# Sums of tokens on another engine and in another block, seven products from block 2 on, later ends, and a weight scale from ScalarE

## The chip, the cores and the metric

The kernel runs on one core of a Trainium2 chip. Five engines work side by side, each with a queue of its own, and wait for one another through semaphores: TensorE (PE; the profile lists its weight loads as PEld), VectorE (DVE), ScalarE (ACT), GpSimd (POOL) and SyncE (SP), which here issues DMA transfers. The metric is the device time of one execution in microseconds, lower is better; the time before is the median of three runs.

## What is computed

With `xn` the rows of `x` brought to mean 0 and variance 1 (2048 tokens, 576 features), the output is `x`, plus the real part of a Fourier transform of `xn` over both axes, plus a two-layer network with 4608 hidden units:

```python
xn = _layernorm(x, axis=-1)
a = jnp.einsum("bsd,ed->bse", xn, dft_hid_re)
b = jnp.einsum("bsd,ed->bse", xn, dft_hid_im)
y = jnp.einsum("ts,bse->bte", dft_seq_re, a) - jnp.einsum("ts,bse->bte", dft_seq_im, b)
h = jnp.maximum(jnp.einsum("bsd,df->bsf", xn, w1), 0)
return x + y + jnp.einsum("bsf,fd->bsd", h, w2)
```

All is float32. The kernel forms each float32 product from three float16 products: an operand is scaled by a power of two and split into an upper half (`hi`, rounded to float16) and a lower half (`lo`, the rest), and `hi*hi + hi*lo + lo*hi` is added up.

## The kernel before

**Stages.** The network comes first, then the Fourier transform over the features (`dft1`), then that over the tokens (the loop over `units` at the end). The change touches the network alone.

**Tiling of the network.** The hidden units are cut into 9 blocks `b` of 512, the tokens into 4 groups `g` of 512. A step is one pair `(b, g)`; `steps` lists them block by block, and step number `n` is the place in that list. In each step the loop forms the first layer of `(b, g)` and beside it the second layer of the step before (`mlp2`, seven products `n` = 0 to 6 of a scheme that gets a 2x2 block product from seven multiplications instead of eight; each is 12 matmuls of 128x288).

**First layer, two ways.** In block 0 `mlp1_step` forms it plainly: 13 matmuls of 128x512 for each of four slices, and four more on half the rows. `mlp1_out` (L340 to L359) then takes two slices out of PSUM and makes the seven left operands `h` that the second layer reads, among them four sums `S1` to `S4`, each split into halves (L358 on ScalarE, L359 on VectorE). From block 1 on `pair_products` (L413) forms the first layer with seven products as well, `P1` to `P7`, for `first` and `second`, the two halves of a block's hidden units; a product is 6 or 8 matmuls of 128x256. Its function `behind` (L445) does what follows a product: PSUM is read by ScalarE or VectorE, `value` (L440) makes a pair of halves, and after `P4` the ends follow: the upper halves of the sums on ScalarE (L468) and the lower halves on VectorE (L469). The four PSUM banks `banks1` are written in turn, so a product must wait until the one before it in its bank has been read (L447, L452, L454).

**Sums of tokens.** The seven products need sums of halves of `xn` transposed (`xT`). `sums_x` (L389) is a generator that makes four such sums for a group with GpSimd instructions of 128x512 (L400 to L404 and L409) and a ScalarE copy (L407). It writes them over `acc` of the group, which held the output of block 0 until that was sent to DRAM (`spill<-acc`, L515). `tq` strings the generators of the four groups together, and the loop advances it a piece at a time in steps 2 to 5.

**Weights.** `prepare_block(b)` gives a list of small pieces of work for the next block (load, scale, split and sums of `w1` and `w2`); `work()` takes one piece from it. The scale of `w1` comes from the greatest magnitude: two reductions on VectorE for each half (`max_w1`, L113, and L531), then `power`, where GpSimd takes the greatest over the partitions (L119), or in blocks 0 and 1 `power_pe`, which does the same with small matmuls (L156). The scale of `w2` comes from a sum of magnitudes that ScalarE forms in one instruction (`sum_w2`, L585). `split` (L178) has an upper half on ScalarE (L180) and a lower half on VectorE (L181). For blocks past 0, `split_w1b` and `sums_w1` (L568 to L572) make the sums of `w1` that the seven products need.

**Output of the second layer.** ScalarE copies four of the seven products into one of three buffers (L507; the buffers are called `sum` and `dbuf` in the profile), VectorE adds the other three (L509), and GpSimd's queue issues the transfers that add a buffer to DRAM (L511). In block 0 VectorE adds all of them into `acc`.

**Passes.** From step 6 on the loop also runs `passes`: a load of a 512 KB tile `f` of the Fourier matrices (one buffer) and its sum of magnitudes on ScalarE (L846). They are for the scales of the last stage.

**Order.** The framework places instructions: it takes the order of the program text and moves an instruction ahead where its inputs are planned to be there; `tc.issue_after` ties one to another. On each engine the order is then fixed, and an instruction that waits holds up all behind it.

The seven products' schedule in a step, with the places at which work, sums and passes are called:

```python
            for k, (do, q) in enumerate((
                (first, P1), (first, P2), (m, 0), (first, P5), (first, P6), (m, 1), (second, P1),
                (first, P7), (m, 2), (second, P2), (first, P3), (first, P4), (m, 3), (second, P6),
                (m, 4), (second, P5), (second, P7), (m, 5), (m, 6), (second, P3), (second, P4),
            )):
```

Of the kernel before, what the change touches and what calls it, by code (L numbers as in the profile page):

```python
# [38 lines left out]

NW1 = 17  # L40
W1B = NW1 * P
EXPONENT = 0x7F800000
SX = 4.0
EPS = 1e-5
# [3 lines left out]
def kernel(  # L48
# [340 lines left out]
    def sums_x(g):  # L389

        f = mlp.tile([P, 2, 2, GH], F32, tag="first", name=f"t{g}", bufs=1)
        tt = nc.gpsimd.tensor_tensor
        for q, (head, tail) in enumerate((
            ((0, 1), (0, 0)), ((1, 1), None), ((1, 0), None), ((1, 1), (0, 1)),
        )):
            t = f[:, q % 2]
            h, l = halves(g, head)
            if tail:
                h2, l2 = halves(g, tail)
                tt(t, h, h2, ALU.subtract)  # L400
                tt(t, t, l2, ALU.subtract)
            else:
                tt(t, h, f[:, 1 - q % 2], ALU.subtract)
            tt(t, t, l, ALU.add)  # L404
# [4 lines left out]
            tt(lo, t, hi, ALU.subtract)  # L409

    banks1 = []

    def pair_products(b, g, i):  # L413

# [30 lines left out]
        def behind(n):  # L445
# [5 lines left out]
            elif n == P6:  # L451
                nc.scalar.activation(s1, u, AF.Copy)  # L452
            elif n == P5:
                nc.scalar.activation(c22, w, AF.Copy)  # L454
            elif n == P7:
                tt(c22, u, c22, ALU.add)  # L456
                value(A22, c22)
            elif n == P3:
                tt(r21, w, s1, ALU.add)
                nc.scalar.activation(r21, r21, AF.Relu)  # L460
                stt(s3, c11, 0.0, r21, ALU.max, ALU.subtract)
                stt(s1, c22, 0.0, r21, ALU.max, ALU.add)
                stt(s2, c22, 0.0, s3, ALU.max, ALU.subtract)
            elif n == P4:
                value(A12, u)
                stt(s4, u, 0.0, s2, ALU.max, ALU.subtract)  # L466
                hi, lo = (h[:, k, S1 : S4 + 1] for k in range(2))
                order["s"] = nc.scalar.activation(hi, st[:, 1:], AF.Copy).ins  # L468
                order["lo"] = nc.vector.tensor_tensor(lo, st[:, 1:], hi, ALU.subtract).ins  # L469

        def run(n):
            product(n)
# [46 lines left out]
    def max_w1(b, f):  # L519
# [3 lines left out]
            mx["w1", b], sc["w1", b], pw["w1", b] = cell("mw1"), cell("sw1"), cell("pw1")  # L523
        if r == 0:
            mx["f", b] = cell("mf", 2)
            mx["b", i] = small.tile([P, 1], BF16, tag=f"mb{i}", name=f"mb{b}_{i}") if b < 2 else None
        with tc.issue_after(order["acc" if b > 1 else "lo"]) if b else nullcontext():
            magnitude(mx["f", b][:, r : r + 1], raws["w1", b, i][:, r * KT : (r + 1) * KT])
        if r:
            m = mx["w1", b][:, i : i + 1] if b > 1 else mx["b", i]  # L530
            nc.vector.tensor_reduce(m, mx["f", b], AX.X, ALU.max)  # L531

    def later(step):

# [2 lines left out]

    def power_w1(b, i):
        s, p = (t["w1", b][:, i : i + 1] for t in (sc, pw))
        if b > 1:  # L540
            yield from power(s, p, mx["w1", b][:, i : i + 1])
        else:
            power_pe(s, p, mx["b", i])

    def split_w1(b, f):
        i, r = divmod(f, 2)
        k = slice(r * KT, (r + 1) * KT)
        if r == 0:
            w = w1bufs[i].bitcast(F16)[:, : 4 * KT * P]
            w1s[b, i] = w.rearrange("p (n k f) -> p n k f", n=2, f=P)  # L550
        w = w1s[b, i]
        split(w[:, 0, k], w[:, 1, k], raws["w1", b, i][:, k], sc["w1", b][:, i : i + 1])

    def split_w1b(b, i, c):

        if c == 0:
            w = w1bufs[b % 2 * 2 + i].bitcast(F16)
            w1s[b, i] = w.rearrange("p (n k f) -> p n k f", n=2, f=P)
        w, r = w1s[b, i], raws["w1", b, i]
        src = (r[:, :5], r[:, 7:], r[:, :5], r[:, 5:9])[c]  # L560
        k = (slice(0, 5), slice(5, 8), slice(8, 13), slice(13, 17))[c]
        split(w[:, 0, k], w[:, 1, k], src, sc["w1", b][:, i : i + 1])

    def sums_w1(b, i):
        r = raws["w1", b, i]
# [288 lines left out]
    for n in range(2, len(steps)):  # L854
# [16 lines left out]
        if b == NB - 1 and g == 1:  # L871
# [51 lines left out]
    mlp.release()  # L923
# [214 lines left out]
```

## Time and profile before

| | |
|---|---|
| median of three runs | 1365.46 us (1365.22 to 1368.71) |
| the profiled execution | 1367.02 us |
| its span | 1364.9 us |
| mean granted TensorE clock | 0.974 |
| block 0, up to step 4 | 0 to 140.05 us |
| block 1 (steps 4 to 7) | 140.05 to 255.51 us |
| blocks 2 to 8 (steps 8 to 35) | 255.51 to 904.45 us |
| both Fourier stages | 904.45 to 1364.9 us |

The stage borders are the starts of matmuls: that of the first product of a step, which is the first matmul of L435 in it. A row of the view by windows gives a stretch, its length, and for each engine the busy time and the number of instructions, then the granted clock of TensorE as a share of full speed, the busy share of the DMA engines, and GB/s. A row of the timeline gives start and duration in microseconds, engine, line, operation and tiles, and in brackets how long the engine had been idle and what ended that. A row of the groups gives the count, the total busy time and the mean duration in ns, then the idle time ahead of those instructions by releaser. A row of the waits gives the total, the number of times and the longest.

### The profile page before, as it was taken

The page shows a single profiled execution, that of the slowest core. Times are in us where ns is not written, and L with a number is a line of the kernel's source. Part 1 is how long each engine was busy: PE and PEld are TensorE (multiplying, and loading weights), DVE is VectorE, ACT ScalarE, POOL GpSimd, SP SyncE. Part 2 cuts the span into 40 slices and gives each one's busy share as a digit, 9 for nine tenths or more (in the row PEclk, how much of TensorE's full clock was granted, in tenths as well). Part 3 has the DMA queues.
Part 4 walks back from the last instruction along what each step waited for, and adds up shares of the span by engine and source line. Part 5 has one row for each costly group of instructions (what it writes and reads, how often), then busy time and mean ns, then how long its engine had stood idle before and what let it go on. Part 6 is the DMA issues. An engine that isn't in the chain of part 4 may idle for free.

```text
span 1364.9 us, 25952 instructions
## 1 busy us (share of the span) xinstructions
PE 1270.6 (93%) x10572; PEld 1023.3 (75%) x10572; DVE 1030.5 (76%) x1911; ACT 725.1 (53%) x1226; POOL 221.1 (16%) x244
## 2 busy tenths in 40 slices
PE   8878689999998999999989999999999999999998
PEld 7654467877877778778778778776777777777777
DVE  8968888677766777877677678648667878788785
ACT  6734346666665576676565666535443433333342
POOL 2466541111111112111111111120000000000000
PEclk8899899999999999999999999999999999999999
DMA  5111225566656647575656676442004443443420
GB/s 213 40 44 53 87 72 98 126 145 142 123 125 147 119 107 158 123 155 115 140 130 119 129 151 150 61 64 82 4 1 146 156 138 101 150 132 115 159 80 18
DMA packets 60807, 150.77 MB, mean 110 GB/s; under 512 B 6288, under 2 KB 21136, under 8 KB 60688
## 3 DMA queue, kind: packets, MB, share of 16 engines
q1 hardware_dynamic: 42256, 111.36, 25.1%
q0 software_dynamic: 18432, 37.76, 19.9%
q8 instruction: 82, 1.34, 0.4%
q14 instruction: 37, 0.30, 0.1%
HBM read 101.91 MB, written 47.19 MB: 109 GB/s over the span
## 4 chain that ended last, share of the span: by engine, by line
PE 43%; issue 18%; DVE 16%; DMA 11%; ACT 6%; POOL 4%; SPq 0%; POOLq 0%; ACTq 0%; DVEq 0%
PE p L1072 23%; PE p L498 7%; PE pd L958 6%; PE bank L435 6%; DMA spill<-dbuf 4%; DVE w2s L181 2%; POOL spill L511 2%; DMA spill<-sum 2%; DMA f<-in_cim_dram 2%; ACT f L846 1%; DVE h L443 1%; DMA c<-in_cre_dram 1%; DMA f<-in_cre_dram 1%; ACT j L585 1%; DVE h L469 1%
## 5 line engine op out<-in xcount | busy, mean ns | idle before, releaser
L498 PE MATMUL p<-w2s,h 128*128 128x288 f16 x3024 | 423.8, 293 | 28.9 <-DVE sum L509 9.3
L498 PEld LDWEIGHTS <-h 128*128 128x128 f16 x3024 | 302.1, 100 | 112.1 <-issue 32.5
L1072 PE MATMUL p<-R,cs 128*128 128x288 f16 x2688 | 331.1, 287 | 2.9 <-DVE o L1078 2.9
L1072 PEld LDWEIGHTS <-cs 128*128 128x128 f16 x2688 | 263.6, 98 | 70.2 <-issue 3.1
L180 ACT ACTIVATE cs<-c,sc_c 128x1024 f16<-128x1024 f32 x112 | 128.8, 1151 | 198.5 <-PE p L1072 152.4
L435 PEld LDWEIGHTS <-dbuf 128*128 128x128 f16 x1600 | 158.5, 99 | 48.5 <-issue 24.8
L435 PEld LDWEIGHTS <-w1buf 128*128 128x128 f16 x1600 | 157.2, 98 | 40.2 <-issue 18.6
L181 DVE SCALAR_TENSOR_TENSOR cs<-c,sc_c,cs 128x1024 f16<-128x1024 f32 x112 | 143.7, 1283 | 46.8 <-ACT cs L180 46.7
L435 PE MATMUL bank<-acc,dbuf 128*128 128x256 f16 x768 | 107.7, 277 | 21.0 <-ACT s L452 20.8
L435 PE MATMUL bank<-acc,w1buf 128*128 128x256 f16 x768 | 105.9, 275 | 15.7 <-ACT s L452 15.6
L511 POOL DMA_DIRECT2D spill<-dbuf x74 | 66.4, 922 | 331.7 <-DVE dbuf L509 327.7
L435 PE MATMUL bank<-xT,dbuf 128*128 128x256 f16 x832 | 112.3, 276 | 0.9 <-DVE s L466 0.9
L435 PE MATMUL bank<-xT,w1buf 128*128 128x256 f16 x832 | 110.4, 274 | 0.7 <-ACT acc L454 0.7
L958 PE MATMUL pd<-dbuf,xT 128*128 128x288 f16 x832 | 104.3, 286 | 1.6 <-DVE R L987 1.3
L469 DVE TENSOR_TENSOR h<-s,h 128x1024 f16<-128x1024 f32 x64 | 78.5, 1226 | 31.0 <-ACT h L468 30.9
L958 PEld LDWEIGHTS <-xT 128*128 128x128 f16 x832 | 80.7, 98 | 25.5 <-issue 5.5
L468 ACT ACTIVATE h<-s 128x1024 f16<-128x1024 f32 x64 | 67.6, 1056 | 46.4 <-DVE s L466 46.1
L507 ACT ACTIVATE dbuf<-p,c_ub 128x576 f32<-128x576 f32 x74 | 54.4, 735 | 50.8 <-PE p L498 23.7
L442 ACT ACTIVATE h<-acc 128x256 f16<-128x256 f32 x128 | 52.3, 409 | 51.8 <-DVE acc L456 47.6
L846 ACT ACTIVATE f<-f 128x1024 f32<-128x1024 f32 x64 | 66.9, 1045 | 14.6 <-DMA f<-in_cim_dram 9.6
L443 DVE SCALAR_TENSOR_TENSOR h<-acc,h 128x256 f16<-128x256 f32 x128 | 55.4, 433 | 25.1 <-ACT h L442 22.8
L1078 DVE SCALAR_TENSOR_TENSOR o<-p,us_c,o 128x288 f32<-128x288 f32 x112 | 57.5, 514 | 20.4 <-PE p L1072 20.2
(151 smaller groups left out, 1540.9 us busy)
## 6 DMA issues: line engine op xcount, KB each, us to landing
spill<-dbuf POOLq DMA_DIRECT2D x74, 288.0 KB, 5.1
f<-in_cre_dram SPq DMA_DIRECT2D x32, 512.0 KB, 3.8
f<-in_cim_dram SPq DMA_DIRECT2D x32, 512.0 KB, 3.7
c<-in_cre_dram SPq DMA_DIRECT2D x32, 512.0 KB, 4.6
c<-in_cim_dram SPq DMA_DIRECT2D x32, 512.0 KB, 4.8
spill<-sum POOLq DMA_DIRECT2D x38, 288.0 KB, 5.0
raw_w<-in_w_dram SPq DMA_DIRECT2D x17, 640.0 KB, 6.0
raw_w<-in_w_dram SPq DMA_DIRECT2D x18, 576.0 KB, 6.0
```

Source lines behind the costliest of these rows:

```text
L180: nc.scalar.activation(hi, src, AF.Copy, scale=s)
L181: nc.vector.scalar_tensor_tensor(lo, src, s, hi, ALU.mult, ALU.subtract)
L435: nc.tensor.matmul(ps, l, r, start=first and m == 0, stop=m == len(todo) - 1, skip_group_check=not first,)
L443: stt(lo, src, 0.0, hi, ALU.max, ALU.subtract)
L468: order["s"] = nc.scalar.activation(hi, st[:, 1:], AF.Copy).ins
L469: order["lo"] = nc.vector.tensor_tensor(lo, st[:, 1:], hi, ALU.subtract).ins
L498: nc.tensor.matmul(ps[:, c], h[:, x, qa, c * P : (c + 1) * P], w[:, y, qb], start=first and i == 0 and j == 0, stop=i == NQ - 1 and j == 2 ...
L511: nc.gpsimd.dma_start(spill[g, row, col], o, accum_op=ALU.add)
L846: nc.scalar.activation(f, f, AF.Abs, scale=2.0**-10, accum_out=sums_c[:, n, q : q + 1])
L958: nc.tensor.matmul(ps[j], xT[g][:, kx, c * P : (c + 1) * P], dsp[j][:, hl, k], start=(t % 2 == 0 and n == 0), stop=(t % 2 == 1 and n == le ...
L1072: nc.tensor.matmul(ps, w[:, a, k], r[:, c, rq], start=first and k == 0 and j == 0, stop=k == HK - 1 and j == 2, skip_group_check=not first,)
L1078: nc.vector.scalar_tensor_tensor(o, ps, us["c"][:, n : n + 1], o, ALU.mult, ALU.add)
```

## The change

Five things are altered.

- `sums_x` runs on VectorE instead of GpSimd. It is advanced in block 1's steps, eight pieces a step, and the rest in the first step of block 2. (In the order that the framework makes of it, 22 of the 56 instructions stand among the last two groups of block 0, 34 in block 1.)
- Block 1 uses the plain first layer of block 0; the seven products begin with block 2 (`BB`). So `w1` of block 1 is split like that of block 0, without sums, and its scale still comes by `power_pe`.
- The ends of a pair's sums are put on a list, `ends`, and taken from it after places 2, 4, 12 and 14 of the schedule: for `first` in the same step behind `m` 3 and `m` 4, for `second` in the next step behind `m` 0 and `P6`.
- From block 2 on, the scale of `w1` comes from a sum of magnitudes of a whole half (128x1280) on ScalarE, whose by-product is written to the buffer that the split fills later. The two reductions and the small one on VectorE go.
- `work()` is called at other places of the schedule (ten times a step as before; twice for each slice in block 1), and the passes begin in step 9, at places 9 and 18 of every step and 14 of odd ones.

```diff
+BB = 2
...
     def sums_x(g):
...
-        tt = nc.gpsimd.tensor_tensor
+        tt = nc.vector.tensor_tensor
...
-    banks1 = []
+    banks1, ends = [], []
...
                 stt(s4, u, 0.0, s2, ALU.max, ALU.subtract)
-                hi, lo = (h[:, k, S1 : S4 + 1] for k in range(2))
-                order["s"] = nc.scalar.activation(hi, st[:, 1:], AF.Copy).ins
-                order["lo"] = nc.vector.tensor_tensor(lo, st[:, 1:], hi, ALU.subtract).ins
+                ends.extend((end_hi, end_lo))
+
+        hi_s, lo_s = (h[:, k, S1 : S4 + 1] for k in range(2))
+
+        def end_hi():
+            order["s"] = nc.scalar.activation(hi_s, st[:, 1:], AF.Copy).ins
+
+        def end_lo():
+            order["lo"] = nc.vector.tensor_tensor(lo_s, st[:, 1:], hi_s, ALU.subtract).ins
...
+    def sum_w1(b, i):
+
+        if i == 0:
+            mx["w1", b], sc["w1", b], pw["w1", b] = cell("mw1"), cell("sw1"), cell("pw1")
+        w = w1bufs[b % 2 * 2 + i].bitcast(F16)
+        w1s[b, i] = w.rearrange("p (n k f) -> p n k f", n=2, f=P)
+        nc.scalar.activation(
+            w[:, : 2 * KT * P].rearrange("p (k f) -> p k f", f=P), raws["w1", b, i], AF.Abs,
+            scale=2.0**-10, accum_out=mx["w1", b][:, i : i + 1],
+        )
...
     def prepare_w1(b, i):
         p = power_w1(b, i)
+        if b < BB:
+            return [
+                lambda: max_w1(b, 2 * i),
+                lambda: max_w1(b, 2 * i + 1),
+                lambda: later(p),
+            ], [
+                lambda: split_w1(b, 2 * i),
+                lambda: split_w1(b, 2 * i + 1),
+            ]
         return [
-            lambda: max_w1(b, 2 * i),
-            lambda: (max_w1(b, 2 * i + 1), b > 1 and next(p)),
+            lambda: (sum_w1(b, i), next(p)),
+            lambda: None,
             lambda: later(p),
...
-        if b:
+        if b >= BB:
             first, second = (pair_products(b, g, i) for i in range(NQ))
...
                 do(q)
-                if k % 2:
+
+                if k in (2, 4, 12, 14) and ends:
+                    ends.pop(0)()
+                for _ in range({2: 1, 3: 1, 5: 1, 8: 1, 9: 1, 12: 1, 13: 1, 16: 1, 18: 2}.get(k, 0)):
                     work()
-                if n < 6:
-                    k % 2 or next(tq, None)
-                elif k in (5, 11, 20) and (k != 5 or n % 3 == 0) and passes:
+                if n == 2 + NG * BB - 2 and k in (5, 9, 13, 18):
+                    next(tq, None)
+                if n > NG * BB and (k in (9, 18) or k == 14 and n % 2) and passes:
                     passes.pop(0)()
...
-            if g + 1 < NG:
+            if b == 0 and g + 1 < NG:
...
-            for _ in range(3):
+            for _ in range(1 if b else 3):
                 work()
             for q in range(2 * i, min(2 * i + 2, 7)):
                 mlp2(pb, pg, q)
-                for _ in range(2 if q > 3 and n == 2 or q < 2 and n == 3 else n - 2):
+                if b:
                     next(tq, None)
-            for _ in range(3):
+            if b and i == 3:
+                next(tq, None)
+            for _ in range(1 if b else 3):
                 work()
...
     for q in range(7):
         mlp2(*steps[-1], q)
+        if ends:
+            ends.pop(0)()
```

More of the change, by code (lines that the diff above doesn't have):

```diff
@@ L525, in max_w1 @@
             mx["f", b] = cell("mf", 2)
-            mx["b", i] = small.tile([P, 1], BF16, tag=f"mb{i}", name=f"mb{b}_{i}") if b < 2 else None
-        with tc.issue_after(order["acc" if b > 1 else "lo"]) if b else nullcontext():
+            mx["b", i] = small.tile([P, 1], BF16, tag=f"mb{i}", name=f"mb{b}_{i}")
+        with tc.issue_after(order["lo"]) if b else nullcontext():
             magnitude(mx["f", b][:, r : r + 1], raws["w1", b, i][:, r * KT : (r + 1) * KT])
         if r:
-            m = mx["w1", b][:, i : i + 1] if b > 1 else mx["b", i]
-            nc.vector.tensor_reduce(m, mx["f", b], AX.X, ALU.max)
+            nc.vector.tensor_reduce(mx["b", i], mx["f", b], AX.X, ALU.max)
     def later(step):
@@ L539, in power_w1 @@
         s, p = (t["w1", b][:, i : i + 1] for t in (sc, pw))
-        if b > 1:
+        if b >= BB:
             yield from power(s, p, mx["w1", b][:, i : i + 1])
@@ L548, in split_w1 @@
         if r == 0:
-            w = w1bufs[i].bitcast(F16)[:, : 4 * KT * P]
+            w = w1bufs[b % 2 * 2 + i].bitcast(F16)[:, : 4 * KT * P]
             w1s[b, i] = w.rearrange("p (n k f) -> p n k f", n=2, f=P)
@@ L554, in split_w1b @@
     def split_w1b(b, i, c):
-        if c == 0:
-            w = w1bufs[b % 2 * 2 + i].bitcast(F16)
-            w1s[b, i] = w.rearrange("p (n k f) -> p n k f", n=2, f=P)
         w, r = w1s[b, i], raws["w1", b, i]
@@ L877 @@
             ]
-        if b:
+        if b >= BB:
             first, second = (pair_products(b, g, i) for i in range(NQ))
```

## The prediction

> **What bounds the kernel now.** I read the page first, then busy time by stage, then single steps, then who waits for whom. The profiled execution took 1367.0 us, of which its span is 1364.9; the three timed runs have a median of 1365.5.
>
> ```profile
> span 1364.9 us, 25952 instructions
> PE 1270.6 (93%) x10572; PEld 1023.3 (75%) x10572; DVE 1030.5 (76%) x1911; ACT 725.1 (53%) x1226; POOL 221.1 (16%) x244
> ```
>
> TensorE (PE) is the engine to watch, but its 93% is an average. The cuts by stage are: the last two token groups of block 0, block 1, blocks 2 to 8, and the Fourier part. Columns: window, its length, busy time of each engine (instructions), granted clock, DMA share, GB/s.
>
> ```profile
> 75.50:140.00 64.50, 52.20 (x342) 32.49 (x341) 45.65 (x75) 26.43 (x44) 42.53 (x36) 0.92 0.19 66
> 140.05:255.51 115.46, 95.34 (x741) 75.49 (x739) 95.98 (x182) 60.12 (x116) 43.31 (x38) 0.91 0.40 93
> 255.51:904.45 648.94, 609.81 (x5154) 508.32 (x5152) 475.96 (x1044) 410.58 (x795) 105.99 (x136) 0.98 0.60 126
> 904.45:1364.90 460.45, 450.27 (x3670) 354.95 (x3667) 344.37 (x425) 181.58 (x199) 3.82 (x5) 1.00 0.32 98
> ```
>
> The same view by step (one block and one token group), the first three steps of block 1, the first of block 2 and one late step:
>
> ```profile
> 140.05:177.71 37.66, 27.06 (x190) 19.93 (x188) 35.06 (x59) 15.51 (x29) 19.45 (x15) 0.82 0.21 62
> 177.71:209.04 31.33, 25.16 (x186) 19.59 (x184) 26.61 (x50) 14.87 (x29) 16.39 (x14) 0.89 0.34 79
> 209.04:233.89 24.85, 21.69 (x186) 17.98 (x184) 19.37 (x48) 17.49 (x33) 3.80 (x6) 1.00 0.45 87
> 255.51:276.82 21.31, 21.31 (x187) 18.00 (x185) 17.62 (x40) 14.38 (x28) 3.05 (x6) 1.00 0.50 99
> 815.08:836.28 21.20, 21.20 (x186) 18.01 (x184) 16.76 (x31) 12.82 (x25) 3.63 (x6) 1.00 0.67 138
> ```
>
> A step of seven products without a stall takes 21.20 us: PE is busy throughout. So blocks 2 to 8 (28 steps, floor 28 x 21.20 = 593.6) lose 55.3 us, 9.3% of the floor, and block 1 (floor 84.8) loses 30.7 in four steps. There VectorE (DVE) fills 35.06 of 37.66 and 26.61 of 31.33, just where GpSimd (POOL) works 19.45 and 16.39. Its instructions are longer there, too:
>
> ```profile
> 182.76 1.22 POOL L403 TENSOR_TENSOR t<-xT,t 128x512 f32<-128x512 f16 x1
> 184.06 1.21 POOL L404 TENSOR_TENSOR t<-t,xT 128x512 f32<-128x512 f32 x1
> 182.89 1.38 DVE L462 SCALAR_TENSOR_TENSOR s<-acc,s 128x256 f32<-128x256 f32 x1
> 184.19 1.37 DVE L463 SCALAR_TENSOR_TENSOR s<-acc,s 128x256 f32<-128x256 f32 x1
> 187.17 0.41 DVE L466 SCALAR_TENSOR_TENSOR s<-bank,s 128x256 f32<-128x256 f32 x1
> ```
>
> L462 and L463 read two SBUF tiles and end 0.29 us behind a POOL instruction (184.27 against 183.98, 185.56 against 185.27), after 1.38 and 1.37; L466, of the same size, reads PSUM and takes 0.41. Then the waits of PE, the first four from 75 to 255 us, the others from 255 to 905 (total, times, longest):
>
> ```profile
> PE bank L435 <- ACT s L452: 12.7, 5, 7.4
> PE pm L156 <- DVE mb L531: 4.6, 1, 4.6
> PE p L498 <- ACT xT L266: 4.6, 1, 4.6
> PE p L498 <- DVE c_sw L123: 2.9, 1, 2.9
> ...
> PE bank L435 <- ACT s L452: 23.6, 19, 3.3
> PE p L498 <- DVE dbuf L509: 7.6, 4, 1.9
> PE p L498 <- DVE sum L509: 6.9, 5, 1.8
> ```
>
> **The change part by part.** *PE's work in block 1.* Eight products come back: per step 52 matmuls of 128x512 and 4 on half the rows, instead of 100 of 128x256; the 84 of 128x288 stay.
>
> ```profile
> 65.48 6.20 PE L308 MATMUL p<-xT,w1buf 128*128 128x512 f16 x28
> 113.62 0.61 PE L333 MATMUL p<-xT,w1buf 64*128 64x512 f16 x4
> 370.73 1.91 PE L435 MATMUL bank<-xT,dbuf 128*128 128x256 f16 x16
> 372.48 1.63 PE L498 MATMUL p<-w2s,h 128*128 128x288 f16 x12
> ```
>
> One matmul lasts about 0.38, 0.27 and 0.29, so the starts lie (6.20 - 0.38)/27 = 0.216, (1.91 - 0.27)/15 = 0.109 and (1.63 - 0.29)/11 = 0.122 apart. A step costs 52 x 0.216 + 0.4 + 84 x 0.122 = 21.9 against 100 x 0.109 + 84 x 0.122 = 21.2: +0.7 a step, **+2.8** in all, and block 1's floor is 87.6.
>
> *Sums of tokens, from POOL to VectorE.* 56 instructions of 128x512 (14 a group).
>
> ```profile
> L409 POOL TENSOR_TENSOR acc<-t,acc 128x512 f16<-128x512 f32 x16 | 22.4, 1405 | 32.0 <-ACT s L348 11.7 <-DVE s L459 10.1 <-DMA spill<-acc 8.5
> L248 DVE TENSOR_TENSOR dbuf<-dbuf 128x512 f16<-128x512 f32 x1 | 0.7, 684 | 0.0
> L352 DVE SCALAR_TENSOR_TENSOR h<-p,h 128x512 f16<-128x512 f32 x8 | 5.5, 681 | 1.6 <-ACT h L351 1.5
> L181 DVE SCALAR_TENSOR_TENSOR w1buf<-raw_w,c_sw,w1buf 128x640 f16<-128x640 f32 x20 | 18.8, 946 | 3.7 <-ACT w1buf L180 3.7
> ```
>
> At L248's 0.684 they are 38 us of VectorE; at POOL's own 1.405 it would be 79, and I take the first, the same engine and size. In the built order 22 of them stand among block 0's last two groups, 34 in block 1. VectorE in a step of block 1 then has: outputs 2 x (0.41 + 0.68 + 4 x 0.41 + 1.22) = 7.9, sums 34/4 x 0.684 = 5.8, three L509 at 0.81 = 2.4 (1.22 and 0.81 are L469's and L509's rows below), and a quarter of block 2's weights, 32 instructions between L466's 0.41 and L181's 0.95, about 5. That is 21.1 by durations, some 18 by starts (L466's successor starts 0.34 behind it, not 0.41): 83% of 21.9, the share that the step at 255.51 carries (17.62 of 21.31) with 0.1 lost. So I give block 1 the loss of blocks 2 to 8, 9.3%: 87.6 x 1.093 = 95.7 instead of 115.5, **-20**. Ends: no loss, -28; the 17% of the step at 209.04 (24.85 over 21.2), 102.5, -13.
>
> The rule that weighs here is the Trainium skill's, page "TensorE: Matmul & The Clock Gate", section "What's actually happening": PE falls to half clock after about 3.4 us of idleness, so a shorter new stall costs only itself. The trace differs: the step at 177.71 has a granted clock of 0.89 and PE busy for 25.16, though its longest wait is the 2.9 us for c_sw. By the rule block 1's remaining 8 us would be waits alone, by the row up to half as much again, 4 us; both lie inside the ends above.
>
> *Block 0's last groups.* VectorE gets 22 x 0.684 = 15.0 there, loses the sums of block 1's w1 and half its splits (about 6.7), and what it waited for POOL. Two PE waits have POOL behind them: ScalarE's copies to xT stand behind L407, which waits for POOL's t, and mb L531 stands behind VectorE's long instructions. Of these 9.2 us I count half, **-5**; ends -11 and +8 (VectorE's net 15.0 - 6.7 on the path).
>
> The sums' last instruction, L411 now, also brings VectorE a wait that POOL had: for spill<-acc to land, 8.5 us in all on the sixteen L409. Behind it in VectorE's queue stand the outputs and L509s that PE waits for. The same on VectorE would cost up to 8.5; in the built order five other instructions and one transfer lie between block 0's last add and the first L411, as on POOL, so I count nothing and keep 8.5 within block 0's upper end.
>
> *Ends made later, in blocks 2 to 8.* In the built order ScalarE's h is hardly moved, but VectorE's lower half now stands behind L509 where it stood ahead of it:
>
> ```profile
> 413.21 1.22 DVE L469 TENSOR_TENSOR h<-s,h 128x1024 f16<-128x1024 f32 x1
> 414.34 0.81 DVE L509 SCALAR_TENSOR_TENSOR dbuf<-p,c_ub,dbuf 128x576 f32<-128x576 f32 x1
> 415.21 1.63 PE L498 MATMUL p<-w2s,h 128*128 128x288 f16 x12 [1.91 <-DVE dbuf L509]
> ```
>
> PE waits 1.91 for an L509 with 1.22 of L469 ahead of it. Nine such waits make 14.5; 1.1 off eight of them is **-9**. What is late next is h itself, first read by the third product of the next step, several us later.
>
> *w1's scale.* Seven blocks lose 28 L113 and 14 small reductions on VectorE and gain 14 sums of 128x1280 with a read each on ScalarE.
>
> ```profile
> L113 DVE TENSOR_REDUCE c_mf<-raw_w 128x1 f32<-128x640 f32 x36 | 29.0, 808 | 0.6 <-DMA raw_w<-in_w_dram 0.5
> L585 ACT ACTIVATE j<-raw_w 128x1152 f32<-128x1152 f32 x16 | 18.7, 1168 | 1.1 <-DMA raw_w<-in_w_dram 0.5 <-DVE h L469 0.4
> L585 ACT ACTIVATION_READ_ACCUMULATOR j<-raw_w 128x1 f32 x16 | 3.1, 197 | 0.0
> ```
>
> VectorE: 28 x 0.81 + 14 x 0.15 = 24.7 less. ScalarE: 1.168 x 1280/1152 + 0.197 = 1.49, x14 = 20.9 more, at 410.58 of 648.94 busy; an idle third covers it, and were it all on the path it would cost 20.9. The 23.6 us in which PE waits for L452 are ScalarE held by late L507s, which wait for spills that leave late behind VectorE: I count a quarter, **-6**. Ends for blocks 2 to 8 together: -55 (no loss) and +21; value -15.
>
> Loads and order: the passes over the Fourier matrices now start at step 9, not 6, with 2.5 a step for 2.33; the Fourier part itself is unchanged, 0.
>
> Sum: -20 - 5 - 15 = -40 (the +2.8 is in block 1's floor): 1367.0 - 40 = **1327 us**, some 38 below the median.
>
> **The rivals.** *A, the ends do nothing* (20%). ScalarE's order is nearly as before and VectorE finds the next instruction equally late; blocks 2 to 8 keep 648.9: 1367 - 25 = 1342. *B, VectorE binds block 1* (12%): durations 21.1 rather than starts count and every wait for ScalarE adds; block 1 loses 22% (107), block 0 gains nothing: 1367 - 8.5 - 15 = 1344. *C, nearly all waits go* (12%): two thirds of the 55.3 and block 1 at 91: 1367 - 37 - 24 - 5 = 1301. *D, slower: the passes block ScalarE* (9%). In odd steps a pass now stands behind product 14 and the next behind 18, with one buffer.
>
> ```profile
> L846 ACT ACTIVATE f<-f 128x1024 f32<-128x1024 f32 x64 | 66.9, 1045 | 14.6 <-DMA f<-in_cim_dram 9.6 <-DMA f<-in_cre_dram 4.8
> 423.72 6.49 DMA f<-in_cre_dram
> f<-in_cre_dram SPq DMA_DIRECT2D x32, 512.0 KB, 3.8
> ```
>
> Between them PE has 14 x 0.109 + 24 x 0.122 = 4.5 us of work. A pass (1.05 + 0.19) and the next load (3.8, or 6.5 as at 423.72) need 5.0 to 7.7, so ScalarE stands 0.5 to 3.2 us before the evacuations behind it. In 14 odd steps that is 7 to 45; the kernel gets slower from 2.9 us each on, and at 3.2 it takes 1372. Against it: until now such waits sum to 14.6 us in 64 passes, and PE has m5 and m6 to do meanwhile.
>
> **How the numbers follow.** The forecast has 47%, and 3% of it and of A and B end within the bound. The range 1306 to 1350 takes in A, B and block 1's ends, and leaves out D's far end and most of C. Faster by over 0.3% (4 us, about what can be told from no change): 0.88; within: 0.03; slower: 0.09.
>
> **What would show it.** Block 1 near 96 us at a clock of about 1.0 (B: over 105, VectorE above 90%); no DVE instruction of 128x256 at 1.37; L498's waits for L509 down from 14.5 to about 5 (A: unchanged); waits of ScalarE for f under 20 us (D: over 40). PE has 10396 matmuls. A block 1 above 110 us or blocks 2 to 8 above 660 makes the prediction wrong.

## The result

The changed kernel takes 1320.93 us (median of four runs, 1319.47 to 1322.33) where the kernel before, run beside it, takes 1365.34 (1363.39 to 1368.71): a ratio of 0.967, 95% interval 0.965 to 0.970. That is 44.4 us less; the forecast was 40 (1327 us from the profiled 1367.0).

### The profile after

The head of the page of the changed kernel:

```profile
span 1320.3 us, 25521 instructions
PE 1252.5 (95%) x10396; PEld 994.1 (75%) x10396; DVE 999.3 (76%) x1879; ACT 726.7 (55%) x1218; POOL 148.2 (11%) x188
```

As block 1 has no seven products any more, both kernels are cut anew here, at the first matmul of the second layer for group 1 of block 0, group 3 of block 0, group 3 of block 1 and group 3 of block 8. The first stretch is block 0's last groups, the second block 1, the third the 28 steps of blocks 2 to 8, the fourth what is left. The view by windows, before:

```profile
83.25:142.12 58.87, 47.05 (x299) 28.61 (x298) 41.31 (x71) 23.91 (x42) 37.12 (x29) 0.91 0.18 62
142.12:257.04 114.92, 94.96 (x739) 75.49 (x737) 95.51 (x182) 59.03 (x113) 43.08 (x38) 0.91 0.41 93
257.04:904.45 647.41, 608.28 (x5140) 506.94 (x5138) 474.67 (x1041) 409.60 (x792) 105.62 (x135) 0.98 0.60 126
```

and after, with the same columns (length, then busy time of PE, PEld, DVE, ACT, POOL, then granted clock, DMA share, GB/s):

```profile
80.48:129.70 49.22, 46.60 (x310) 27.57 (x308) 46.63 (x95) 24.93 (x42) 0.00 (x0) 1.00 0.20 68
129.70:215.93 86.23, 85.79 (x552) 52.62 (x551) 80.61 (x156) 45.59 (x74) 11.64 (x15) 1.00 0.43 92
215.93:862.76 646.83, 603.57 (x5140) 505.12 (x5138) 454.84 (x1005) 424.46 (x822) 105.76 (x136) 0.99 0.60 131
862.76:1320.30 457.54, 448.78 (x3670) 354.34 (x3667) 344.02 (x425) 181.05 (x199) 3.81 (x5) 1.00 0.32 99
```

So the gain sits early: 2.8 us ahead of the first border, 9.7 in block 0's last groups, 28.7 in block 1, then 0.6 in blocks 2 to 8 and 2.9 in the rest, 44.7 together against 44.6 between the spans. (These borders lie some microseconds into a step, where plain and seven products have done different amounts of work. The prediction's border, the first product of a step, splits the first two otherwise; the last part comes back to that.) Block 1 is as good as without a loss: 86.23 us, of which PE is busy for 85.79, at full clock. VectorE is busy there for 80.61, 93%, and yet PE hardly waits for it.

The waits of PE after the change, the first four rows from 75 to 214 us, the others from 214 to 863:

```profile
PE p L506 <- DVE acc L517: 1.7, 3, 0.7
PE p L310 <- ACT xT L265: 1.2, 1, 1.2
PE p L506 <- ACT h L360: 0.4, 1, 0.4
PE pm L158 <- DVE mb L538: 0.2, 1, 0.2
...
PE bank L437 <- ACT s L454: 32.2, 20, 5.1
PE bank L437 <- ACT acc L449: 6.7, 6, 1.7
PE p L506 <- DVE sum L517: 1.5, 2, 0.8
PE p L506 <- DVE dbuf L517: 1.5, 2, 0.8
```

(L437, L454, L449, L506 and L517 are the L435, L452, L447, L498 and L509 of before.) Early, the waits for mb and xT have gone from 4.6 us each to 0.2 and 1.2. In blocks 2 to 8 the second layer's waits for VectorE have gone from 14.5 to 3.0, and the seven products' waits for ScalarE have gone from 24 to 39: one wait has taken the other's place.

What ScalarE itself waits for in blocks 2 to 8, after:

```profile
ACT f L870 <- DMA f<-in_cim_dram: 22.5, 11, 3.7
ACT f L870 <- DMA f<-in_cre_dram: 20.4, 8, 4.5
ACT sums L515 <- DMA spill<-sums: 3.9, 2, 3.4
ACT dbuf L515 <- DMA spill<-dbuf: 0.4, 2, 0.3
```

It stands 42.9 us before the loads of the passes, where it stood 14.4 before (9.6 and 4.8 in the prediction's row of L846). How that reaches PE, in the timeline of the changed kernel:

```profile
440.44 1.04 ACT L870 ACTIVATE f<-f 128x1024 f32<-128x1024 f32 x1
...
448.13 1.06 ACT L870 ACTIVATE f<-f 128x1024 f32<-128x1024 f32 x1 [3.40 <-DMA f<-in_cim_dram]
...
453.30 1.04 ACT L870 ACTIVATE f<-f 128x1024 f32<-128x1024 f32 x1
454.34 0.37 ACT L456 ACTIVATE acc<-bank 128x256 f32<-128x256 f32 x1
454.61 0.38 ACT L454 ACTIVATE s<-bank 128x256 f32<-128x256 f32 x1
455.03 0.82 PE L437 MATMUL bank<-acc,w1buf 128*128 128x256 f16 x6 [1.92 <-ACT s L454]
```

The pass at 440.44 has to be over before the next load may fill the one buffer, and the next pass comes up 4.3 us behind its start. ScalarE is held 3.40 us by that load, all that is queued behind it runs late, a second pass stands in the same queue at 453.30, and the copy L454 that frees a bank comes last. PE waits 1.92 for it.

### The profile page after: what moved, and what is told of

Same layout as the page of the kernel before. It is cut to its first block, busy times and chain, and to the rows that moved or that the text cites. A ratio compares the mean times of both kernels' runs of the same rounds, so it can differ in the third digit from the quotient of the medians.

```text
span 1320.3 us, 25521 instructions
## 1 busy us (share of the span) xinstructions
PE 1252.5 (95%) x10396; PEld 994.1 (75%) x10396; DVE 999.3 (76%) x1879; ACT 726.7 (55%) x1218; POOL 148.2 (11%) x188
## 4 chain that ended last, share of the span: by engine, by line
PE 52%; DVE 10%; DMA 10%; issue 9%; ACT 8%; POOL 1%; SPq 0%; ACTq 0%; POOLq 0%; DVEq 0%
PE p L1103 24%; PE p L506 10%; PE bank L437 9%; PE pd L989 6%; DMA f<-in_cim_dram 4%; DMA f<-in_cre_dram 3%; ACT f L870 3%; PE p L310 2%; DVE w2s L183 2%; DMA raw_w<-in_w_dram 1%; POOL spill L519 1%; DMA c<-in_cre_dram 1%; ACT h L474 1%; DVE h L445 1%; ACT j L600 1%
## 5 line engine op out<-in xcount | busy, mean ns | idle before, releaser
L506 PE MATMUL p<-w2s,h 128*128 128x288 f16 x3024 | 409.9, 288 | 7.6 <-DVE acc L517 1.7
L506 PEld LDWEIGHTS <-h 128*128 128x128 f16 x3024 | 296.7, 98 | 87.4 <-issue 8.9
L437 PEld LDWEIGHTS <-w1buf 128*128 128x128 f16 x1600 | 157.5, 98 | 46.2 <-issue 24.5
L183 DVE SCALAR_TENSOR_TENSOR cs<-c,sc_c,cs 128x1024 f16<-128x1024 f32 x112 | 143.7, 1283 | 44.7 <-ACT cs L182 44.5
L437 PEld LDWEIGHTS <-dbuf 128*128 128x128 f16 x1200 | 117.3, 98 | 35.6 <-issue 20.2
L437 PE MATMUL bank<-acc,w1buf 128*128 128x256 f16 x768 | 106.1, 275 | 21.2 <-ACT s L454 19.6
L437 PE MATMUL bank<-xT,w1buf 128*128 128x256 f16 x832 | 110.9, 274 | 0.7 <-ACT acc L456 0.7
L437 PE MATMUL bank<-acc,dbuf 128*128 128x256 f16 x576 | 78.5, 272 | 17.9 <-ACT s L454 12.6
L477 DVE TENSOR_TENSOR h<-s,h 128x1024 f16<-128x1024 f32 x56 | 68.6, 1224 | 26.9 <-ACT h L474 26.7
L437 PE MATMUL bank<-xT,dbuf 128*128 128x256 f16 x624 | 82.3, 273 | 0.0
L474 ACT ACTIVATE h<-s 128x1024 f16<-128x1024 f32 x56 | 59.1, 1055 | 34.9 <-DVE s L468 34.9
L444 ACT ACTIVATE h<-acc 128x256 f16<-128x256 f32 x112 | 45.9, 410 | 51.6 <-DVE acc L458 33.6
L1109 DVE SCALAR_TENSOR_TENSOR o<-p,us_c,o 128x288 f32<-128x288 f32 x112 | 57.5, 514 | 19.9 <-PE p L1103 19.9
L515 ACT ACTIVATE dbuf<-p,c_ub 128x576 f32<-128x576 f32 x74 | 54.1, 732 | 22.6 <-PE p L506 17.6
L445 DVE SCALAR_TENSOR_TENSOR h<-acc,h 128x256 f16<-128x256 f32 x112 | 47.3, 422 | 23.1 <-ACT h L444 23.1
```

Source lines behind the costliest of these rows:

```text
L183: nc.vector.scalar_tensor_tensor(lo, src, s, hi, ALU.mult, ALU.subtract)
L437: nc.tensor.matmul(ps, l, r, start=first and m == 0, stop=m == len(todo) - 1, skip_group_check=not first,)
L445: stt(lo, src, 0.0, hi, ALU.max, ALU.subtract)
L474: order["s"] = nc.scalar.activation(hi_s, st[:, 1:], AF.Copy).ins
L477: order["lo"] = nc.vector.tensor_tensor(lo_s, st[:, 1:], hi_s, ALU.subtract).ins
L506: nc.tensor.matmul(ps[:, c], h[:, x, qa, c * P : (c + 1) * P], w[:, y, qb], start=first and i == 0 and j == 0, stop=i == NQ - 1 and j == 2 ...
```

## The experiments

Each kernel is the changed one with the edit shown, unless it says "before". The table has the lengths of the three stretches in the profiled execution, the median, and the ratio to the kernel before run beside it (95% interval). One execution of each is profiled, and executions of one kernel differ (those of c1 go from 1293.8 to 1305.3 us, and the profiled one is the fastest), so a few microseconds between two stretches can be chance.

| kernel | block 0's last groups | block 1 | blocks 2 to 8 | median us | ratio |
|---|---|---|---|---|---|
| before | 58.9 | 114.9 | 647.4 | 1365.3 | 1 |
| changed | 49.2 | 86.2 | 646.8 | 1320.9 | 0.967 (0.965 to 0.970) |
| e1 sums on GpSimd | 58.5 | 106.1 | 650.6 | 1355.0 | 0.994 (0.992 to 0.996) |
| e2 before, sums on VectorE | 47.1 | 116.1 | 645.2 | 1350.3 | 0.991 (0.988 to 0.994) |
| e3 ends at once | 49.9 | 86.2 | 642.0 | 1322.8 | 0.971 (0.968 to 0.975) |
| e4 w1's scale from VectorE | 49.8 | 85.6 | 666.8 | 1343.7 | 0.986 (0.982 to 0.990) |
| e5 no loads for the passes | 49.6 | 86.2 | 609.7 | 1286.0 | 0.942 (0.939 to 0.945) |
| e6 passes spaced evenly | 49.6 | 86.3 | 640.6 | 1316.3 | 0.965 (0.961 to 0.969) |
| e8 old places of work | 49.2 | 86.0 | 646.1 | 1324.0 | 0.970 (0.966 to 0.974) |
| e9 old places of the passes | 49.8 | 86.3 | 624.2 | 1302.7 | 0.954 (0.951 to 0.958) |
| c1 e9 and ends at once | 48.7 | 86.2 | 619.9 | 1298.4 | 0.953 (0.949 to 0.957) |
| c2 e9 and w1's scale from VectorE | 49.6 | 85.6 | 647.8 | 1323.1 | 0.971 (0.967 to 0.974) |
| c3 e9 and block 3 prepared later | 49.3 | 86.2 | 626.2 | 1301.5 | 0.954 (0.950 to 0.958) |
| c6 e9 and extra maxima | 49.1 | 86.2 | 646.1 | 1317.7 | 0.968 (0.965 to 0.971) |

### The engine of the sums, and block 1's products

```diff
-        tt = nc.vector.tensor_tensor
+        tt = nc.gpsimd.tensor_tensor
```

> The changed kernel with the sums of tokens made by GpSimd again, all else as changed (block 1 plain, ends later, w1's scale from ScalarE). Theory: of the 28.7 us that block 1 lost less after the change, most came from GpSimd no longer holding VectorE up, whatever products block 1 uses; so block 1 loses 10 to 25 us of them again (its stretch 96 to 111 us in place of 86), many of VectorE's reads of the first layer's results take 1 us or more, the rest stays: 1331 to 1346. Rival: it is the plain products of block 1, with fewer results to take out for each product, that ended the loss, and the engine of the sums is nothing: 1318 to 1324, the stretch at 86.

```diff
 the kernel before:
-        tt = nc.gpsimd.tensor_tensor
+        tt = nc.vector.tensor_tensor
```

> The kernel before with one edit: the sums of tokens made by VectorE in place of GpSimd, at their old places in block 0's last groups and the start of block 1. Theory (GpSimd held VectorE up): block 0's last groups and block 1 get most of their 38 us back, so 1328 to 1348. Rival (VectorE binds there once it makes the sums too, and only the move of the sums into a plain block 1 frees it): block 1's stretch stays over 108 us, 1358 to 1372.

Block 0's last groups go with the engine alone: 58.9 and 58.5 with GpSimd, 47.1 and 49.2 with VectorE. Block 1 does not: with seven products VectorE's sums bring nothing (114.9 to 116.1), plain products with GpSimd's sums bring 8.8 (106.1), and both together 28.7. So e1's theory has the size for block 1 (19.9 us, of 10 to 25 expected) and missed block 0's groups, 9.3 more, which it took to stay; e2's is right for block 0 and wrong for block 1, where its rival is, and 1350.3 lies between the two. In e2 VectorE has more to do in block 1 than fits: 99.90 us, where the prediction's floor for these steps is 84.8. In the changed kernel it has 80.61, which fits. The rows of e2's view by windows (block 1, and its second quarter, in which VectorE is busy for 28.99 of 29.00):

```profile
126.64:242.77 116.13, 93.28 (x727) 73.46 (x725) 99.90 (x213) 61.53 (x114) 12.15 (x15) 0.93 0.40 93
...
156.00:185.00 29.00, 23.45 (x187) 17.97 (x186) 28.99 (x61) 14.80 (x28) 1.88 (x2) 1.00 0.23 62
```

In e1 it is another queue that binds. The second quarter of its block 1 in the view by windows:

```profile
168.00:195.00 27.00, 14.41 (x62) 7.97 (x61) 10.32 (x14) 9.95 (x17) 20.20 (x17) 0.70 0.20 53
```

The longest of ScalarE's waits in its block 1 (141 to 247 us):

```profile
ACT acc L409 <- POOL t L406: 23.0, 6, 6.4
```

And its timelines of GpSimd, ScalarE and PE:

```profile
176.79 5.86 PE L506 MATMUL p<-w2s,h 128*128 128x288 f16 x24 [7.72 <-ACT sum L515]
...
187.34 1.15 POOL L406 TENSOR_TENSOR t<-t,xT 128x512 f32<-128x512 f32 x1
188.53 0.63 ACT L409 ACTIVATE acc<-t 128x512 f16<-128x512 f32 x1 [6.36 <-POOL t L406]
189.06 0.58 ACT L353 ACTIVATE h<-p 128x512 f16<-128x512 f32 x1
189.54 0.73 ACT L515 ACTIVATE dbuf<-p,c_ub 128x576 f32<-128x576 f32 x1
190.32 5.94 PE L506 MATMUL p<-w2s,h 128*128 128x288 f16 x24 [4.87 <-ACT dbuf L515]
```

ScalarE rounds each sum (L409) between two pieces of GpSimd, so it stands 6.36 us for GpSimd, with the first layer's output (L353) and the second layer's (L515) queued behind; PE waits 4.87 for the latter. The price of GpSimd here is mostly ScalarE's place in the queue. GpSimd also comes late: its L411 at 144.03 had waited 13.8 us for spill<-acc to land, and no run tells how much of the rest follows from that. That GpSimd stretches VectorE's instructions, as the expectation had it, is seen in e1 where they read two SBUF tiles: the splits of w1 with 128x512 take 1192 ns on the mean, against 753 in the changed kernel, and two sums of w1 with 128x256 (L585 and L586) 836 and 840 against 424 and 426. The outputs L355 to L358 read one tile in PSUM and one in SBUF and have their usual 0.41 us, so the reads that the expectation counted on do not grow with plain products. Over e1's block 1 PE waits 13.3 us, and its busy time is 92.74 us at a granted clock of 0.92, where the changed kernel has 85.79 at 1.00: together about the 19.9. In the quarter shown the granted clock is 0.70 with waits of 7.72 and 4.87 us. The Trainium skill's page "TensorE: Matmul & The Clock Gate", section "What's actually happening", puts the fall to half clock behind about 3.4 us of idleness; this quarter agrees with it.

### The later ends

```diff
             elif n == P4:
...
-                ends.extend((end_hi, end_lo))
+                end_hi()
+                end_lo()
```

> The changed kernel with the two ends of a pair's sums made directly behind the pair's last product, as before; all else as changed. Theory (the later ends do take away waits, and ScalarE's waits for its loads and w1's sums give that back): the second layer's matmuls wait for VectorE's copies and sums again, 10 us or more in place of 3, so blocks 2 to 8 take 657 to 667 us in place of 649 and the kernel 1328 to 1340. Rival (the later ends are worth nothing, since both ends only stand where VectorE and ScalarE had time): 1317 to 1324.

The same edit on top of e9 (below), where the loads are out of the way:

> The changed kernel with two parts undone: the sums over the transform's inputs at their old places (which alone gave 1302.7 us) and the ends of a pair's sums made at once. Theory one (the later ends gain what the forecast said, 9 us, and it was covered before by ScalarE's waits for loads): 1308 to 1316, with waits of L507, the second layer's matmuls, over 8 us. Theory two (the later ends gain nothing here either): 1299 to 1306.

The later ends gain nothing that shows in either place (the rival of e3, theory two of c1): with the ends at once blocks 2 to 8 take 642.0 in place of 646.8, and 619.9 in place of 624.2, and the ratios overlap. The waits that were to come back do so in part, as e3's rows for 214 to 870 us show:

```profile
PE bank L437 <- ACT s L454: 26.3, 16, 3.3
PE bank L437 <- ACT acc L449: 4.8, 6, 1.5
PE p L507 <- DVE dbuf L518: 4.3, 3, 1.9
...
PE p L507 <- DVE sum L518: 0.7, 2, 0.5
```

The second layer (here L507) waits 5.0 us for VectorE instead of 3.0, and the products' waits for ScalarE at L454 and L449 fall from 38.9 to 31.1. What the later ends take away at one place comes in at the other.

### w1's scale

```diff
...
-            lambda: (sum_w1(b, i), next(p)),
-            lambda: None,
+            lambda: max_w1(b, 2 * i),
+            lambda: (max_w1(b, 2 * i + 1), next(p)),
```

> The changed kernel with w1's scale of blocks 2 to 8 from VectorE's maxima again, in two steps of the list of work, all else as changed. Theory one (ScalarE's sums over w1 stand ahead of the copies that free banks, and cost what the later ends gain): the first step of each block loses less, blocks 2 to 8 take 640 to 646 us, the kernel 1312 to 1318. Theory two (the sums on ScalarE cost about as much there as the maxima cost on VectorE): 1318 to 1325. Theory three (taking the maxima from VectorE is what removed its waits of 14.5 us): 1326 to 1335.

> The changed kernel with two parts undone: the sums over the transform's inputs at their old places (which alone gave 1302.7 us) and w1's scale of blocks 2 to 8 from VectorE's maxima. Theory one (the 22.8 us that the maxima cost with the new places came of the scale ready later, the splits and the next load of w behind it, and that load among the loads of the transform's inputs; with the old places they do not meet so): 1302 to 1311. Theory two (w1's scale from ScalarE is worth about 20 us by itself, whatever the places): 1318 to 1328.

Blocks 2 to 8 take 20.0 us more in e4 (666.8 against 646.8) and 23.6 more in c2 (647.8 against 624.2): theory two of c2, above the range of all three theories of e4. To see whether it is VectorE's work or the moment at which the scale is there, the last run keeps ScalarE's sum and makes the maxima as well, for nobody:

```diff
...
-            lambda: (sum_w1(b, i), next(p)),
-            lambda: None,
+            lambda: (sum_w1(b, i), next(p), extra_max(b, 2 * i)),
+            lambda: extra_max(b, 2 * i + 1),
```

> The changed kernel with the sums over the transform's inputs at their old places (1302.7 us by itself) and, beside ScalarE's sum of w1, VectorE's maxima of w1 made again for blocks 2 to 8, 28 instructions of 0.81 us whose results nobody reads. Theory one (VectorE's time is what w1's scale from ScalarE saved: the maxima stand ahead of VectorE's reads of banks): most of the 20 us come back, 1315 to 1326. Theory two (the scale being ready some 3 us earlier is what counts, since the splits and the next load of w follow it): 1299 to 1308, and the next load of w is issued as early in its step as without the maxima. Between them, 1309 to 1314, both have a part.

21.9 us come back in the profiled executions (646.1 against 624.2; c6's is the slowest of its six, and by the medians it is 15.0, by the ratios about 19). 24 of the 28 extra maxima lie in these blocks, 24 x 0.81 = 19.4 us by their durations and 16.6 of VectorE's busy time. ScalarE's sum costs nothing that shows: c6, which makes the sum and the maxima, is no slower than c2, which makes the maxima alone. It is not settled whether each microsecond of VectorE counts or what it makes late: in c6 the scale, the splits and the load of w2's block behind them come later, too. In block 4 that load is issued 20.6 us into its step (424.54, step from 403.91), against 15.9 in e9 (414.81, from 398.95). There it starts among the spills (issued at 421.63, 424.01 and 424.61; in e9 the first of them is issued at 415.76, behind the load). ScalarE's waits for spills in c6's blocks 2 to 8:

```profile
ACT dbuf L515 <- DMA spill<-dbuf: 11.9, 5, 3.5
ACT sum L515 <- DMA spill<-sum: 10.5, 3, 3.6
ACT sums L515 <- DMA spill<-sums: 2.0, 1, 2.0
```

and the row of its 576 KB loads in the view of the DMA issues (their median time to landing is last):

```profile
raw_w<-in_w_dram SPq DMA_DIRECT2D x12, 576.0 KB, 7.2
```

24.4 us of waits for spills and 7.2 to landing, where e9 has 6.7 and 3.9 (its rows stand below). The kernel before (24.5 and 6.1), e4 (29.2 and 7.0) and c2 (33.9 and 8.0) are like c6, the changed kernel (4.3 and 4.0) is like e9.

### The passes and the list of work

The sums over the transform's inputs without their loads but the first, at the same places:

```diff
-        f = firsts[m] = mlp.tile([P, HK, P], F32, tag="first", name=f"f{n}_{q}", bufs=1)
-        nc.sync.dma_start(f, blocks_c(n)[q])
+        if m == 0:
+            firsts[-1] = mlp.tile([P, HK, P], F32, tag="first", name=f"f{n}_{q}", bufs=1)
+            nc.sync.dma_start(firsts[-1], blocks_c(n)[q])
+        firsts[m] = firsts[-1]
...
-                f, f, AF.Abs, scale=2.0**-10, accum_out=sums_c[:, n, q : q + 1]
+                f, f, AF.Abs, accum_out=sums_c[:, n, q : q + 1]
```

> The changed kernel in which the 64 sums over the transform's inputs keep their places on ScalarE but only the first of the 64 loads is made: all sums run over that one array, so the scale of the last stage comes from part of the data. Theory (ScalarE's waits for these loads, 43 us in blocks 2 to 8, stand ahead of the copies that free banks): the waits of the matmuls at L437 fall from 39 to 10 to 20 us, blocks 2 to 8 take 620 to 632 us in place of 649 and the kernel 1290 to 1305. Rival (these waits end together with others that stay, such as the sums' own 1.24 us or the second layer's copies): 1312 to 1321.

This leaves the theory's range on the good side: blocks 2 to 8 take 609.7, 37.1 us less and 16 above the floor of 593.6 that the prediction gives, and PE's waits for the copies at L454 fall to 12.5:

```profile
PE bank L437 <- ACT s L454: 12.5, 11, 4.7
```

The 64 sums are still made there, 1.24 us each and 79 in all, so most of their time is hidden; that of the loads is not. As e5 also takes 63 loads off the DMA engines (their share falls from 0.60 to 0.50), it does not tell ScalarE's waits from the traffic. The next two runs change only the places, with the same loads:

```diff
-                if n > NG * BB and (k in (9, 18) or k == 14 and n % 2) and passes:
+                if n > NG * BB and k in ((4, 11, 18) if n % 2 else (7, 18)) and passes:
```

> The changed kernel with only the places of the sums over the transform's inputs changed: after products 4, 11 and 18 of odd steps and 7 and 18 of even ones, so that seven or more products (7 us) lie between two of them in place of four or five. Theory: the loads take 4.5 to 8 us, so most land in time, ScalarE's waits for them fall from 43 to 5 to 20 us, and blocks 2 to 8 take 630 to 645 us, the kernel 1302 to 1317. Rival (a wait only moves to the next in line): 1318 to 1325.

```diff
-                if n > NG * BB and (k in (9, 18) or k == 14 and n % 2) and passes:
+                if (n > 8 and k in (5, 11, 20) and (k != 5 or n % 3 == 0 or n == 10) or n == 8 and k == 20) and passes:
```

> The changed kernel with the sums over the transform's inputs after products 5 (every third step), 11 and 20 again, as before, all else as changed. Theory (the new places, four and five products apart, are what lets ScalarE wait 43 us for loads, against 14 before): these waits fall under 20 us, blocks 2 to 8 take 630 to 645 us, the kernel 1302 to 1317. Rival (the places were moved with the rest for a reason and waits for spilled sums come back): 1320 to 1335.

With the old places blocks 2 to 8 take 624.2, 22.6 us less and under the theory's range. The longest wait of PE there, and ScalarE's waits for loads and spills:

```profile
PE bank L437 <- ACT s L454: 19.4, 17, 3.9
...
ACT f L870 <- DMA f<-in_cim_dram: 13.3, 7, 5.2
ACT f L870 <- DMA f<-in_cre_dram: 8.4, 5, 2.8
ACT dbuf L515 <- DMA spill<-dbuf: 5.3, 7, 2.8
ACT sums L515 <- DMA spill<-sums: 1.4, 1, 1.4
```

Its window, and behind it, from the DMA issues, the row of the 576 KB loads:

```profile
215.12:839.33 624.21, 601.16 (x5140) 504.65 (x5138) 456.11 (x1005) 425.29 (x822) 105.25 (x136) 0.99 0.63 136
```

```profile
raw_w<-in_w_dram SPq DMA_DIRECT2D x12, 576.0 KB, 3.9
```

The waits for the passes' loads halve, from 42.9 to 21.7 (not quite under the 20 expected), and hardly any other wait takes their place. (The old places begin here at the end of step 8, in the kernel before in step 6.) e6 does less (640.6, 6.3 us, and its ratio overlaps that of the changed kernel): there the waits for loads fall to 28.1, but ScalarE waits for spills again, 16.5 us (8.8, 4.8 and 2.9). And its passes are evenly spaced in the program text only. Each is tied behind the copy of the upper halves of the sums (`tc.issue_after(order["s"])`), and in the queue pairs still stand close, such as this one of e6, 4.5 us apart without the wait:

```profile
382.13 1.05 ACT L870 ACTIVATE f<-f 128x1024 f32<-128x1024 f32 x1
...
389.43 1.06 ACT L870 ACTIVATE f<-f 128x1024 f32<-128x1024 f32 x1 [2.76 <-DMA f<-in_cre_dram]
```

Of the 63 passes that follow another, those that come up less than 6 us behind the start of the one before are 7 in the kernel before, 12 in e9, 17 in e6 and 19 in the changed kernel, and at them stand 11.9 of 14.4, 19.5 of 21.7, 27.0 of 28.1 and 40.5 of 42.9 us of the waits for loads. So the distance in the queue goes with these waits, and no run here has spaced the passes evenly; which place suits which other transfer was not taken apart further.

```diff
-                for _ in range({2: 1, 3: 1, 5: 1, 8: 1, 9: 1, 12: 1, 13: 1, 16: 1, 18: 2}.get(k, 0)):
+                for _ in range(k % 2):
```

> The changed kernel with one step of the list of work after every second product again, as before, all else as changed (the sums over the transform's inputs keep their new places). Theory one (the new places only fit the new w1 scale and cost as much as it brings): the kernel within 5 us of the changed one, 1316 to 1326. Theory two (the new places are what keeps w1's scale from standing ahead of copies that free banks): slower, 1328 to 1345, with more waits of L437 for ScalarE.

Theory one in its numbers: 646.1 against 646.8, the same waits. The places of the list of work are worth nothing that shows.

The last edit goes for the first step of block 2, which in e9 still takes 28.2 us in place of 21.2, with ScalarE waiting 3.1 us for w1:

```diff
-            [lambda: (load_w1(b, 0), load_w1(b, 1))] + wait
+            [lambda: (load_w1(b, 0), load_w1(b, 1))] + wait * (2 if b == 3 else 1)
```

> The changed kernel with the sums over the transform's inputs at their old places, and block 3's preparation begun two steps of the list later, so that ScalarE's first sum over w1 in block 2 stands behind the landing of its load. Theory (the 6 to 7 us lost in the first step of block 2 are ScalarE's waits of 3.1 us for that load and what stands behind them): that step loses 2 us or less, 1296 to 1300. Rival (the wait moves to the step where the list has caught up): 1300 to 1305.

The rival's case: that step takes 26.6 us, blocks 2 to 8 626.2 against 624.2, the kernel 1301.5 against 1302.7, no difference that can be told. Of the kernels that compute everything, c1 is the fastest at 1298.4 us, some 20 us below the changed kernel; its lead over e9 is within the intervals.

## Why the prediction was right, and where its sum was not

*Block 1* was forecast at -20. From the first product of its first step to that of block 2, the prediction's border, it now takes 90.19 us in place of 115.46:

```profile
124.21:214.40 90.19, 89.38 (x562) 53.24 (x560) 84.57 (x164) 48.07 (x79) 11.35 (x14) 1.00 0.40 86
```

That is -25.3, towards the end of -28 that the prediction gave for no loss. (The table's borders put 28.7 on block 1 and 9.7 on block 0's last groups; with this border it is 25.3 and 13.1, the same sum.) The mechanism was right: the sums' weight moved to VectorE at 689 ns a piece (0.684 was used), and the plain products left it room, as the groups of VectorE in block 1 show (the outputs, such as L357, are at 419 ns on the mean, and no instruction of that size takes 1.37 us):

```profile
L406 DVE TENSOR_TENSOR t<-t,xT 128x512 f32<-128x512 f32 x9 | 6.2, 689 | 0.2
L411 DVE TENSOR_TENSOR acc<-t,acc 128x512 f16<-128x512 f32 x9 | 6.1, 689 | 0.7 <-ACT acc L409 0.7
L357 DVE SCALAR_TENSOR_TENSOR s<-p,s 128x256 f32<-128x256 f32 x9 | 3.8, 419 | 0.0
```

The mis-sized term is the 9.3% that was carried over from blocks 2 to 8 as a loss: PE is idle for 0.8 of the 90.19 us, 0.9% (against the floor of 87.6 it is 3.0%, as PE's own work came to 89.4). Most of what blocks 2 to 8 lose goes with the loads of the passes (e5: 37.1 of the 53.2 us above the floor), and block 1 has no passes. VectorE's work was 84.57 us, the 21.1 a step that the prediction had by durations, and 94% of the time: the sign named for rival B, without B's loss. B did happen where it was not looked for: in e2, with the seven products kept. What the prediction says of why GpSimd costs was half the story; ScalarE behind L406 is the greater part in e1.

*Block 0's last groups* brought -13.1 by that border for -5, past the end of -11. Both waits named, mb and xT, went almost wholly (9.2 to 1.4 us), where half was counted. The wait of L411 for the spill of acc that was kept in the range is 0.8 us.

*Ends made later*: counted at -9, worth nothing in e3 and c1. The sign came as forecast, the second layer's waits falling from 14.5 to 3.0 us, but they are no measure of the time: e4 has none of them and is slower, e3 has 5.0 and is not. The step that failed is to take a wait of PE that an edit removes for time gained; PE then waited for ScalarE's copies instead.

*w1's scale*: counted at -6, measured at -20 to -24 (e4, c2). The step that failed is "I count a quarter" of 23.6 us. The relief of VectorE was computed (24.7 us), and then only a part of ScalarE's wait was credited; with the maxima back in c6, for nobody, most of the time is back (15.0 us by the medians, 21.9 by the stretches). Whether VectorE's time itself lay on the path, or what came later for it, stays open. ScalarE's 14 sums cost nothing that shows, as said.

*Loads and order*: counted at 0, measured at +22.6 (e9). Here the prediction had the right mechanism and put it among the rivals, D, at 9%. D's sign, waits for f over 40 us, came (42.9, where the forecast said under 20), and where D put it: counted in the order of the calls, 38.6 of the 42.9 us stand at the pass behind product 18 of the odd steps, 3.0 in each of the 13 that have one (D gave 0.5 to 3.2). Its price, 7 to 45 us, holds the 22.6. D was told as a case instead of the forecast, while both were true at once: +22.6 met the -20 to -24 of w1's scale, and blocks 2 to 8 ended at -0.6 where -15 was forecast. That the total came out is luck: block 1 and block 0 brought 13.4 us more than forecast, blocks 2 to 8 14.4 less, and what was set at 0 brought 5.7.

*The rest* was set at 0. Ahead of the first border it is -2.8, of the same kind as block 0's groups: that border lies at 83.3 and 82.7 with GpSimd's sums (before, e1) and at 79.0 to 80.8 in all the runs with VectorE's. The Fourier part, -2.9, is not the change's: e9 and c2, whose Fourier code is the same, differ by 3.1 from each other there (444.8 and 441.8 from the last matmul of the second layer to the last of all).

## What to carry to other kernels

When a stage hardly changes under an edit of five parts, undo the parts one at a time: here two of them, over 20 us each, hid each other, and putting one back made a kernel 18 us faster than the change. On an engine that works in order, price a step that loads into a single buffer by what is queued behind its wait, above all the copies that free the matmuls' banks, and look up in the built order how far apart such steps really stand. An engine that is 93% busy need not bind (block 1), and 17 us of extra work that bring one to 73% can cost the kernel 15 us and more (c6).

## What the runs showed of the hardware that was not expected

With VectorE's busy time in blocks 2 to 8 cut by 17 us (455 to 456 us in the changed kernel and e9, 472 to 473 in e4, c2 and c6), the time fell by 20 to 24 us, though VectorE was busy for only 73% of the stretch (472.7 of 647.8 in c2). And the same twelve 576 KB loads of w2 take a median of 3.9 us in e9 and 8.0 in c2, with a DMA share of 0.63 and 0.59. They start at other moments, in the one load looked at here (e9 against c6) ahead of the 288 KB spills or among them; that this is the cause is argued, not shown.
